# 232 small products of a zero tile at the beginning of an attention and MLP kernel

## The chip, the core and the metric

The kernel runs on one core of a Trainium2 chip. The engines are TensorE (PE in the profile: matmuls; PEld: the loading of their stationary operand), VectorE (DVE), ScalarE (ACT), GpSimd (POOL) and SyncE (SP, which issues most DMAs). Each engine takes its instructions in the order in which the program lists them. The metric is the device time of one launch in microseconds; lower is better. The median of three runs before is 1787.42 us (1785.45 to 1788.26).

## The reference, cut to what matters

The program is a chain of three layers over 8 batches of 576 rows and 512 columns: a landmark (Nyström) attention with 8 heads, a token mixer of rank 32 with an MLP, and a Fourier mixer with a normalisation and a second MLP.

```
q_lm = q.reshape(B, H, 32, 18, D).mean(axis=3);  k_lm = the same of k
A, Bm, C = sm(q, k_lm), sm(q_lm, k_lm), sm(q_lm, k)      # softmax of scaled products
Z = Bm^T / (norm1(Bm) * norminf(Bm));  6 times: Z = 2 Z - Z Bm Z
attn = A @ Z @ C @ v
u = x + (x^T U V)^T;   x1 = u + relu(u @ w_ch1) @ w_ch2
u = x1 + real(fft(fft(x1)));  un = normalised(u)
out = u + relu(un @ w_ch1') @ w_ch2'
```

Only the first few instructions of the first batch's attention lie beside the change: the means of q and k over 18 rows (the landmarks), `Bm` and `C`.

## The kernel before, in words

The whole program is one list written by hand (`tc.manual_schedule()`), so the order of the Python code is the order on each engine. The main part is matrix products of 128x512 tiles for the MLPs, three products for each pair of tiles (high times high, low times high, high times low), on PE without pause for most of the run. The attention of a batch is a chain of small steps, spread over slots between those products. For batch 0 there are no products to fill in yet: the MLP has no input until the attention of batch 0 is done. In its slots the program puts fillers (L1541 to L1543: six products of the identity with itself, read by nobody) and sums for later batches (L738).

What runs first, by engine:

- SP loads k and q of batch 0 (L719, two DMAs each), then constants, then raw weights.
- POOL fills four tiles with zeros in `attention_constants`: `v` (L664), `ETt` (L665), then `kb` and `qb` (L668). `kb` and `qb` are 128x256 tiles that hold the landmarks of k and q in a block pattern; the zeros between the blocks stay for the whole attention part.
- DVE sums k and q over 18 rows (L726, into the small tile `ls`), twice for each. After each sum POOL scales the result into `kb` or `qb` (`landmark`, L728, two instructions for each sum).
- PE then multiplies `qb` by `kb` (`Batch.kernel`, L759: eight products of a 128x32 stationary part of `qb` with a 128x32 part of `kb`, each group of four written to four different 32-row quarters of the result), and `qb` by k (`scores`, L823 and L828). DVE takes the maxima (L765, L831, L833), ACT the exponentials (L767, L837).
- POOL's next work after the landmarks is a conversion step (L69) of the token mixer's matrix U, which DVE's L71 waits for.

A product of two float32 tiles stands in the trace as two records on PE: the eight of L759 are sixteen. `mlp.bank()` hands out three PSUM banks in turn.

Of the kernel before, what the change touches and what calls it, by code (L numbers as in the profile page):

```python
# [9 lines left out]
F32 = mybir.dt.float32  # L10
# [13 lines left out]
P = 128  # L24
# [11 lines left out]
def f32(ap):  # L36
    return ap.bitcast(F32)
# [3 lines left out]
def body(ctx: ExitStack, tc: tile.TileContext, qT, kT, vn, mU, mV, w11, w12, w21, w22,  # L41
         ident, bones, istack, tabs, out):
    nc = tc.nc
# [42 lines left out]
    def fetch_raw(raw, src):  # L86
        nc.sync.dma_start(raw, src.bitcast(U32))
# [568 lines left out]
    UB = 4  # L656

    def attention_constants(cp, t):
        t["ident"] = cp.tile([P, P], F32, name="ident_sb")
        nc.sync.dma_start(t["ident"], ident)  # L660
        t["U"] = cp.tile([P, 6, R], F32, name="U_sb")
        t["v"] = cp.tile([P, 5, DM], F32, name="v_")
        t["ETt"] = cp.tile([P, 2, P], F32, name="ETt")
        nc.gpsimd.memset(t["v"][64:P, 4, :], 0.0)  # L664
        nc.gpsimd.memset(t["ETt"][64:P], 0.0)  # L665
        for nm in ("kb", "qb"):
            t[nm] = cp.tile([P, 4, 64], F32, name=nm)
            nc.gpsimd.memset(t[nm], 0.0)  # L668
        for nm, src, n in (("bones", bones, P), ("istack", istack, R)):
            t[nm] = cp.tile([P, n], F32, name=nm + "_sb")  # L670
            nc.sync.dma_start(t[nm], src)
        t["at"] = cp.tile([P, 4, S], F32, name="at")
        t["W"] = cp.tile([P, 4, 64], F32, name="W")
# [16 lines left out]
    def place_v(t):  # L690
        for n in range(3):
            src = t["vst"][R * n:R * n + R].unsqueeze(1).to_broadcast([R, 2, S // 3])
            for h in range(4):
                nc.sync.dma_start(t["at"][32 * h:32 * h + 32, 1 - h % 2:4:2, n * S // 3:(n + 1) * S // 3], src)
# [622 lines left out]
    def pool(name, **k):  # L1317
        return tc.tile_pool(name=name, bufs=1, reuse_waits="tile", **k)

    def chained(gens):  # L1320
        for g in gens:
            yield from g

    def some(gen, n):
        for _ in range(n):
            next(gen, 0)
# [156 lines left out]
    with pool("mm") as mp, pool("pm", space=PSUM) as pm:  # L1483
        mlp = Mlp(mp, pm, 3, passes)

        def direct():

            ws = [mlp.weight(nm) for nm in ("w1", "w2") for _ in range(HM)]
            raws = []
            seq = [*range(4), *range(HM, 2 * HM, 2), *range(4, HM), *range(HM + 1, 2 * HM, 2)]  # L1490

            def fetch():
                i = len(raws)
                if i < len(ws):
                    if i < EARLY:
                        raw = f32(mp.tile([P, 2, 512], F32R, name="g", bufs=HM)).rearrange(
                            "p a n -> p (a n)").bitcast(U32)
                    else:
                        raw = cv0.tile([P, 1024], U32, name="wraw", bufs=2)
                    fetch_raw(raw, srcs[0][seq[i]])  # L1500
                    raws.append(raw)

            for n in range(2):
                fetch()
                yield 1

            old = None
            for n, i in enumerate(seq):
                while len(raws) < min(max(n + 2, min(n + 3, EARLY)), len(ws)):
                    fetch()  # L1510
                new = convert(cv0, raws[n], ws[i], 2)
                for g in (new, old, old, new):
                    if g:
                        yield next(g)
                old = new
            yield from old

        EARLY = 8
        with pool("aa") as ap_, pool("ac") as ac, pool("cv0") as cv0, pool("pt", space=PSUM) as psb:
            t = {}  # L1520
            batches = [Batch(ap_, psb, t, b, mlp) for b in range(B)]
            slots = Slots()
            FIRST, GAP = -1 - Batch.LAST, 11
            half = (0, 1, 2, 4, 6, 8, 9, 10)
            for b in range(B):
                slots.add(GAP + STEPS * (b - 1) - 23 + 2 * (b == 1) if b else FIRST, batches[b].steps(batches[b + 1] if b + 1 < B else None))
            slots.add(GAP + STEPS * (B - 1) - 10, [(0, lambda: mlp.get_tail(B))])
            slots.add(GAP + STEPS * (B - 1) - 8, ((k, lambda k=k: mlp.hand_tail(B, k)) for k in range(4)))

            slots.add(FIRST, [(11, lambda: place_v(t))])  # L1530

            sums = {**{n - 11: [(1, 'k', 3 * n, 3 * n + 3)] for n in range(6)}, 3: [(2, 'k', 0, 6)], 5: [(2, 'k', 6, 12)], 7: [(2, 'k', 12, 18)]}

            def filler(s):

                if s in sums:
                    for b, nm, first, last in sums[s]:
                        batches[b].landmark_sums(nm, first, last)
                    return

                ps = mlp.bank()  # L1541
                for _ in range(6):
                    nc.tensor.matmul(ps[:, 0:P], t["ident"], t["ident"], start=True, stop=True)  # L1543

            with tc.manual_schedule():
                for what in "kq":
                    batches[0].load(what)
                attention_constants(ac, t)
                small, large = attention_setup(t, ap_, cv0), direct()
                some(small, 1)  # L1550
                some(large, 1)
                batches[0].load("v")
                some(large, 1)
                convs = chained([small, large])
                for s in range(FIRST, 0):
                    slots.run(s)
                    if s - FIRST in (6, *range(10, 20)):
                        filler(s)
                    some(convs, 0 if s < FIRST + 4 else 1 + s % 2)
                later, gen = staging(cv0, 1, 2), mlp.stream(0)  # L1560
                for s in range(N + GAP - 8):
                    if s >= GAP or s in half:
                        next(gen)
                    else:
                        filler(s)
                    slots.run(s)
                    if s < GAP + 13:
                        some(convs, 2)
                        if s == GAP + 12:
                            some(convs, 99)  # L1570
                    else:
                        some(later, 1 if s % 3 == 2 else 2)
                some(later, 999)
                some(gen, 9)
        with tc.manual_schedule():
            scales = Scales(rs)
            mlp.plan(UN, [(c, c + 1) for c in range(PLAIN, NCH, 2)], quarters)
            with pool("cv") as cv, pool("fp") as fp, pool("fc") as fc, pool("pf", space=PSUM) as psb:
                f = {}
                slots = Slots()  # L1580
                starts = (33, 58, 83, 108, 133, 157, 182, 206)
                for b, s in enumerate(starts):
                    slots.add(s, Mixer(fp, psb, f, b).steps(b + 1 == B))
                later = Pace(chained([staging_pairs(cv, (2, 3)), staging_sums(cv)]))
                gen = mlp.stream(1)
                setup = fourier_setup(f, fc, fp)

                def room(s):
                    r = s - max((a for a in starts if a <= s), default=-99)
                    return 1.45 if r > 40 else 1.4 if r in (*range(10, 21), 23, 24) else .7 if r in (4, 9, 21, 22) else 0  # L1590

                for s in range(N + 2 * PLAIN * STEPS - LEAD):
                    if s in (N, N + PLAIN * STEPS):
                        some(gen, 9)
                        gen = mlp.stream(2 + (s > N))
                    next(gen)
                    slots.run(s)
                    next(setup, 0)
                    later.step(room(s))
                later.rest()  # L1600
            assert not slots.at
            with pool("tl") as mlp.last_pool, pool("tp", space=PSUM) as mlp.last_ps:
                last = mlp.pairs(quarters, Y, scales, U2, ByChunk(y3))
                next(last)
                for s in range(LEAD):
                    next(gen)
                    next(last)
                    next(last)
                some(gen, 9)
                for _ in last:  # L1610
                    pass
# [83 lines left out]
```

## Time and profile before

| | |
|---|---|
| median of three runs | 1787.42 us |
| lowest, highest | 1785.45, 1788.26 us |
| profiled execution: its time | 1789.14 us |
| profiled execution: span of the core | 1787.4 us |
| mean granted TensorE clock | 0.997 |
| PE busy | 1757.6 us (98%) |
| DVE busy | 1171.2 us (66%) |
| POOL busy | 328.2 us (18%) |

The span goes from the core's first to its last instruction; the time of the execution is 1.7 us longer. Where the profile holds no record of the granted clock it shows 1.00: the first 15 us of this run have none, and there the durations of PE's own records must be read instead. Matmuls of one engine overlap, so the distance between starts, not the duration of one record, is what a record costs in a sequence.

### The profile page before, as it was taken

What the parts mean: (1) busy time and instruction counts of PE and PEld (TensorE: products, weight loads), DVE (VectorE), ACT (ScalarE), POOL (GpSimd) and SP (SyncE); (2) the same over time, 40 slices, a digit from 0 to 9 for tenths busy, and PEclk for the clock granted to TensorE, in tenths of its full rate; (3) what the DMA queues carried; (4) which work ended last, traced back from release to release, by engine and by line L of the source; (5) the groups of instructions that cost most, each with busy time, mean ns of one, the idle gap of its engine ahead of it and who ended that gap; (6) DMA issues with size and microseconds to landing.
All of it is one profiled execution on the core that took longest, in us unless ns stands there. A gap on an engine that the chain in (4) does not pass through costs nothing.

```text
span 1787.4 us, 30912 instructions
## 1 busy us (share of the span) xinstructions
PE 1757.6 (98%) x11905; PEld 1432.7 (80%) x11905; DVE 1171.2 (66%) x2028; ACT 735.6 (41%) x1520; POOL 328.2 (18%) x314
## 2 busy tenths in 40 slices
PE   6999999999999999999999999999999999999999
PEld 4777777777788888888878888888878888888887
DVE  7897666566322977888886665657575674577564
ACT  4554443444211333433342333434256445454642
POOL 3324211221110321211111122211111001100100
PEclk9999999999999999999999999999999999999999
DMA  7555456443536764546555954776688778878764
GB/s 254 182 174 171 152 175 206 155 162 105 179 137 249 242 234 154 183 164 216 179 179 193 329 200 148 273 281 201 222 290 273 216 243 257 261 228 247 223 214 153
DMA packets 215895, 371.00 MB, mean 208 GB/s; under 512 B 28970, under 2 KB 129930, under 8 KB 215748
## 3 DMA queue, kind: packets, MB, share of 16 engines
q1 hardware_dynamic: 211140, 359.59, 60.9%
q10 hardware_dynamic: 4608, 9.44, 1.4%
q8 instruction: 94, 1.54, 0.4%
q14 instruction: 53, 0.43, 0.1%
HBM read 262.18 MB, written 106.17 MB: 206 GB/s over the span
## 4 chain that ended last, share of the span: by engine, by line
PE 88%; DVE 7%; DMA 2%; ACT 1%; issue 1%; SPq 0%; POOL 0%; DVEq 0%; ACTq 0%
PE ps L291 9%; PE ps L293 9%; PE ps L292 9%; PE ps L238 9%; PE ps L240 8%; PE ps L239 8%; PE ps L329 7%; PE ps L331 7%; PE ps L330 7%; PE ps L554 1%; PE ps L553 1%; PE ps L555 1%; PE ps_f L77 1%; PE ps_f L76 1%; PE ps_f L75 1%
## 5 line engine op out<-in xcount | busy, mean ns | idle before, releaser
L238 PE MATMUL ps<-x,w 128*128 128x512 f32 x768 | 305.4, 398 | 0.2 <-DVE g L243 0.2
L291 PE MATMUL ps<-g,w 128*128 128x512 f32 x768 | 304.2, 396 | 0.0
L240 PE MATMUL ps<-x,w 128*128 128x512 f32 x768 | 299.8, 390 | 0.0
L293 PE MATMUL ps<-g,w 128*128 128x512 f32 x768 | 299.8, 390 | 0.0
L239 PE MATMUL ps<-x,w 128*128 128x512 f32 x768 | 299.4, 390 | 0.0
L292 PE MATMUL ps<-g,w 128*128 128x512 f32 x768 | 299.2, 390 | 0.0
L243 DVE SCALAR_TENSOR_TENSOR g<-ps,g 128x512 fp32r<-128x512 f32 x192 | 132.4, 690 | 206.7 <-ACT g L242 206.4
L242 ACT ACTIVATE g<-ps 128x512 fp32r<-128x512 f32 x192 | 114.0, 597 | 264.0 <-PE ps L240 263.4
L291 PEld LDWEIGHTS ps<-g,w 128*128 128x128 f32 x768 | 144.3, 188 | 31.9 <-issue 3.5
L240 PEld LDWEIGHTS ps<-x,w 128*128 128x128 f32 x768 | 144.1, 188 | 31.4
L293 PEld LDWEIGHTS ps<-g,w 128*128 128x128 f32 x768 | 144.1, 188 | 31.1
L238 PEld LDWEIGHTS ps<-x,w 128*128 128x128 f32 x768 | 144.3, 188 | 29.9 <-DVE g L243 0.6
L292 PEld LDWEIGHTS ps<-g,w 128*128 128x128 f32 x768 | 144.4, 188 | 27.4
L239 PEld LDWEIGHTS ps<-x,w 128*128 128x128 f32 x768 | 144.4, 188 | 26.9
L302 DVE TENSOR_TENSOR xf<-ps,xf 128x512 f32<-128x512 f32 x88 | 60.5, 687 | 86.7 <-PE ps L293 84.6
L406 ACT COPY ps<-ps 128x512 f32<-128x512 f32 x126 | 72.4, 575 | 94.4 <-PE ps L331 93.4
L51 POOL TENSOR_TENSOR stg<-cva,stg 128x512 fp32r<-128x512 f32 x48 | 65.4, 1363 | 216.8 <-ACT stg L50 190.4
L458 POOL TENSOR_TENSOR w<-w,w 128x512 f32<-128x512 f32 x24 | 33.3, 1389 | 362.1 <-DMA w<-rs 181.6
L329 PE MATMUL ps<-xs,w 128*128 128x512 f32 x240 | 94.2, 392 | 1.9 <-ACT ps L406 1.9
L331 PE MATMUL ps<-xs,w 128*128 128x512 f32 x240 | 94.1, 392 | 0.0
L330 PE MATMUL ps<-xs,w 128*128 128x512 f32 x240 | 93.9, 391 | 0.0
L51 POOL TENSOR_TENSOR x<-xf,x 128x512 fp32r<-128x512 f32 (+7 forms) x48 | 60.1, 1254 | 157.9 <-ACT x L50 122.7
(420 smaller groups left out, 3356.9 us busy)
## 6 DMA issues: line engine op xcount, KB each, us to landing
w<-e SPq DMA_DIRECT2D x84, 512.0 KB
w<-d SPq DMA_DIRECT2D x126, 256.0 KB
w<-d SPq DMA_DIRECT2D x60, 512.0 KB
wraw<-w SPq DMA_DIRECT2D x56, 512.0 KB
d<-stg SPq DMA_DIRECT2D x48, 512.0 KB
y<-xf SPq DMA_DIRECT2D x64, 256.0 KB
xf<-y SPq DMA_DIRECT2D x52, 256.0 KB
u<-u1T ACTq DMA_DIRECT2D x32, 288.0 KB
```

The lines of the kernel that those rows point to most:

```text
L51: (eng or nc.vector).tensor_tensor(lo, src, f32(hi), op=ALU.subtract)
L238: nc.tensor.matmul(ps, wh, xh, start=k == 0, stop=False)
L239: nc.tensor.matmul(ps, wl, xh, start=False, stop=False)
L240: nc.tensor.matmul(ps, wh, xl, start=False, stop=k == 3)
L242: nc.scalar.activation(g[:, 0, :], ps, AF.Relu)
L243: nc.vector.scalar_tensor_tensor(out=g[:, 1, :], in0=ps, scalar=0.0, in1=f32(g[:, 0, :]), op0=ALU.max, op1=ALU.subtract)
L291: nc.tensor.matmul(ps, wh, gh, start=k == m0, stop=False)
L292: nc.tensor.matmul(ps, wl, gh, start=False, stop=False)
L293: nc.tensor.matmul(ps, wh, gl, start=False, stop=k == m1 - 1)
L329: nc.tensor.matmul(ps, wh, xh, start=first and k == 0, stop=False, skip_group_check=True)
L330: nc.tensor.matmul(ps, wl, xh, start=False, stop=False, skip_group_check=True)
L331: nc.tensor.matmul(ps, wh, xl, start=False, stop=last and k == 1, skip_group_check=True)
```

## The change

Three things are edited. The zero fill of `qb` and `kb` moves to the head of `attention_constants`, ahead of those of `v` and `ETt`, with `qb` first. Then, after the constants and ahead of everything else that PE does, 232 products are issued. Each takes columns 0 to 31 of `qb` as the stationary operand and columns 32 to 63 as the moving one, both over 128 rows, and writes the same 32x32 corner of one PSUM bank. Nobody reads the result. `qb` holds zeros at that time.

```diff
--- before.py
+++ after.py
@@ -656,6 +656,9 @@
     UB = 4
 
     def attention_constants(cp, t):
+        for nm in ("qb", "kb"):
+            t[nm] = cp.tile([P, 4, 64], F32, name=nm)
+            nc.gpsimd.memset(t[nm], 0.0)
         t["ident"] = cp.tile([P, P], F32, name="ident_sb")
         nc.sync.dma_start(t["ident"], ident)
         t["U"] = cp.tile([P, 6, R], F32, name="U_sb")
@@ -663,9 +666,6 @@
         t["ETt"] = cp.tile([P, 2, P], F32, name="ETt")
         nc.gpsimd.memset(t["v"][64:P, 4, :], 0.0)
         nc.gpsimd.memset(t["ETt"][64:P], 0.0)
-        for nm in ("kb", "qb"):
-            t[nm] = cp.tile([P, 4, 64], F32, name=nm)
-            nc.gpsimd.memset(t[nm], 0.0)
         for nm, src, n in (("bones", bones, P), ("istack", istack, R)):
             t[nm] = cp.tile([P, n], F32, name=nm + "_sb")
             nc.sync.dma_start(t[nm], src)
@@ -1515,7 +1515,7 @@
                 old = new
             yield from old
 
-        EARLY = 8
+        EARLY, WARM = 8, 232
         with pool("aa") as ap_, pool("ac") as ac, pool("cv0") as cv0, pool("pt", space=PSUM) as psb:
             t = {}
             batches = [Batch(ap_, psb, t, b, mlp) for b in range(B)]
@@ -1546,6 +1546,9 @@
                 for what in "kq":
                     batches[0].load(what)
                 attention_constants(ac, t)
+                ps, warm = mlp.bank(), t["qb"].rearrange("p a m -> p (a m)")
+                for _ in range(WARM):
+                    nc.tensor.matmul(ps[0:32, 0:32], warm[:, 0:32], warm[:, 32:64], start=True, stop=True)
                 small, large = attention_setup(t, ap_, cv0), direct()
                 some(small, 1)
                 some(large, 1)
```

On PE before, the program begins with the products of the landmarks (`ps_b` is a PSUM bank of the attention):

```order
L759 MATMUL ps_b<-kb,qb 32x32 [waits Pool_49] x2
L759 MATMUL ps_b<-kb,qb 32x32 x2
L759 MATMUL ps_b<-kb,qb 32x32 [waits Pool_49]
L759 MATMUL ps_b<-kb,qb 32x32 x3
L823 MATMUL ps_c<-k__226,qb 32x512 [waits DMAHW0_49]
```

In the changed kernel the 232 products (`ps<-qb`) stand ahead of the same list:

```order
L1551 MATMUL ps<-qb 32x32 [waits Pool_49]
L1551 MATMUL ps<-qb 32x32 x231
L759 MATMUL ps_b<-kb,qb 32x32 [waits Pool_49] x2
L759 MATMUL ps_b<-kb,qb 32x32 x2
L759 MATMUL ps_b<-kb,qb 32x32 [waits Pool_49]
L759 MATMUL ps_b<-kb,qb 32x32 x3
L823 MATMUL ps_c<-k__605,qb 32x512 [waits DMAHW0_49]
```

All that PE had in its list before comes behind the 232 products, in the same order.

On POOL before, the zero fills and the landmark scalings read so (`ls` is the sum that DVE made):

```order
L664 MEMSET v__235 64x512
L665 MEMSET ETt 64x256
L668 MEMSET kb 128x256 [waits Pool_49]
L668 MEMSET qb 128x256
L677 MEMSET wraw 128x128
L728 ISA
L728 TENSOR_SCALAR kb<-ls 64x2x32 [waits DVE_49,Pool_49]
L728 TENSOR_SCALAR kb<-ls 64x2x32 [waits Pool_49]
L728 TENSOR_SCALAR kb<-ls 64x2x32 [waits DVE_49]
L728 TENSOR_SCALAR kb<-ls 64x2x32
L728 TENSOR_SCALAR qb<-ls 64x2x32 [waits DVE_49]
```

In the changed kernel, the same stretch:

```order
L661 MEMSET qb 128x256
L661 MEMSET kb 128x256
L667 MEMSET v__239 64x512 [waits Pool_49]
L668 MEMSET ETt 64x256
L677 MEMSET wraw 128x128
L728 ISA
L728 TENSOR_SCALAR kb<-ls 64x2x32 [waits DVE_49]
L728 TENSOR_SCALAR kb<-ls 64x2x32 [waits Pool_49]
L728 TENSOR_SCALAR kb<-ls 64x2x32 [waits DVE_49]
L728 TENSOR_SCALAR kb<-ls 64x2x32
L728 TENSOR_SCALAR qb<-ls 64x2x32 [waits DVE_49,PE_49]
```

The fill of `qb` is now POOL's first work after the start, and the first scaling into `qb` has a new wait, on PE: it overwrites what the 232 products read.

## Rows read from the trace of the kernel before

**Rows 1.** The page: busy time by engine, and the chain by engine.

```profile
PE 1757.6 (98%) x11905; PEld 1432.7 (80%) x11905; DVE 1171.2 (66%) x2028; ACT 735.6 (41%) x1520; POOL 328.2 (18%) x314
...
PE 88%; DVE 7%; DMA 2%; ACT 1%; issue 1%; SPq 0%; POOL 0%; DVEq 0%; ACTq 0%
```

**Rows 2.** Timeline of POOL: start us, us, engine, line, operation, count, [idle before <-releaser].

```profile
0.73 0.52 POOL L664 MEMSET v__235<- 64x512 f32 x1 [0.29 <-POOLq L1684]
...
1.81 0.33 POOL L668 MEMSET qb<- 128x256 f32 x1
...
8.95 0.81 POOL L728 TENSOR_SCALAR qb<-ls 64x64 f32<-64x64 f32 x2 [0.86 <-DVE ls L726]
10.42 0.85 POOL L728 TENSOR_SCALAR qb<-ls 64x64 f32<-64x64 f32 x2 [0.65 <-DVE ls L726]
```

**Rows 3.** Timeline of PE, same columns, 0 to 60 us.

```profile
9.37 0.77 PE L759 MATMUL ps_b<-kb,qb 128*32 128x32 f32 x8 [9.37 <-POOL qb L728]
11.32 0.34 PE L759 MATMUL ps_b<-kb,qb 128*32 128x32 f32 x8 [1.18 <-POOL qb L728]
11.59 1.96 PE L823 MATMUL ps_c<-k__226,qb 64*32 64x512 f32 x16
...
13.69 2.35 PE L1543 MATMUL ps<-ident_sb 128*128 128x128 f32 x12
...
23.75 0.65 PE L969 MATMUL ps_n<-ry 32*32 32x64 f32 x16 [3.75 <-DVE cva L95]
24.33 1.11 PE L851 MATMUL ps_c<-ident_sb,E 128*128 128x128 f32 x4
...
33.85 0.66 PE L928 MATMUL ps_c<-ident_sb,A 128*128 128x128 f32 x4
...
38.95 0.46 PE L951 MATMUL ps_b<-U_sb,A 128*32 128x32 f32 x32
...
42.84 1.60 PE L1543 MATMUL ps<-ident_sb 128*128 128x128 f32 x12
...
44.73 1.09 PE L823 MATMUL ps_c<-k__372,qb 64*32 64x512 f32 x16
```

**Rows 4.** The chain that ended last, 0 to 24 us: start us, us, what.

```profile
11.66 1.91 PE ps_c L823 x16
...
13.59 1.29 DVE st L831 x2
```

**Rows 5.** Timeline of DVE, columns as in rows 2.

```profile
13.21 0.15 DVE L778 TENSOR_TENSOR st<-st 128x2 f32<-128x2 f32 x1
```

**Rows 6.** One line's PE records: duration ns min/median/max, first and last start.

```profile
L951 PE MATMUL ps_b<-U_sb,A x64: 196/196/217, 38.9 to 39.6; 128*32 128x32 f32 x64
...
L1543 PE MATMUL ps<-ident_sb x60: 274/275/581, 13.7 to 55.0; 128*128 128x128 f32 x60
...
L851 PE MATMUL ps_c<-ident_sb,E x8: 421/421/474, 24.3 to 28.1; 128*128 128x128 f32 x8
...
L928 PE MATMUL ps_c<-ident_sb,A x8: 272/272/328, 33.9 to 37.0; 128*128 128x128 f32 x8
```

**Rows 7.** Windows: busy us (instructions) of PE, PEld, DVE, ACT, POOL; PEclk, DMA share, GB/s.

```profile
0.00:5.00 5.00, 0.00 (x0) 0.00 (x0) 0.58 (x1) 1.28 (x1) 1.69 (x9) 1.00 0.63 219
...
20.00:25.00 5.00, 1.25 (x19) 1.11 (x20) 4.05 (x14) 0.84 (x2) 0.00 (x0) 0.71 0.99 372
25.00:30.00 5.00, 5.00 (x37) 4.28 (x35) 4.83 (x10) 2.86 (x6) 1.32 (x1) 0.61 0.54 165
28.00:29.00 1.00, 1.00 (x7) 0.93 (x6) 0.93 (x4) 0.47 (x1) 0.00 (x0) 0.53 0.14 41
29.00:30.00 1.00, 1.00 (x6) 0.80 (x5) 0.97 (x3) 1.00 (x3) 0.00 (x0) 1.00 0.13 37
...
60.00:1787.40 1727.40, 1714.94 (x11042) 1399.84 (x11040) 1124.26 (x1917) 707.28 (x1444) 310.52 (x284) 1.00 0.62 206
```

**Rows 8.** Waits of PE after 60 us: us in total, times, longest.

```profile
PE ps_l L1255 <- DVE le L1250: 2.7, 3, 1.4
```

## The prediction, made before the run

> **What bounds the kernel now.** I read the page first: PE is busy for 98% of the span and holds 88% of the chain that ended last [rows 1]. The windows say where the rest is: PE does nothing in the first 5 us, and after 60 us it is idle for only 1727.40 - 1714.94 = 12.5 us [rows 7]. So from 60 us on PE runs almost without pause, and what moves its work of the first microseconds moves the end by about the same amount. Then the timelines of POOL and PE for the beginning, with the chain. PE's first instruction starts at 9.37 us, released by POOL's scaling into `qb`; the second half of the same eight products follows at 11.32 us, after POOL's second pair of scalings, which starts at 10.42 and takes 0.85 us [rows 2, 3]. From there the chain goes through L823 to DVE's maximum at 13.59 us [rows 4]. DVE had ended the step before it (L778) at 13.21 + 0.15 = 13.36 us [rows 5], so only 0.23 us of that stretch waits for PE alone.
>
> The clock needs a second look. In the first windows the profile shows 1.00 only because it has no record. L1543's twelve records take 2.35 us at 13.69 and 1.60 us at 42.84; L823's sixteen 1.96 us at 11.59 and 1.09 us at 44.73 [rows 3]. [...]
>
> **The change part by part.** The new zero fills cost nothing: the same five fills, with `qb` first. PE can begin when that one is done, at 0.73 + 0.33 us, and 0.05 us for the handover (POOL ends at 10.42 + 0.85 = 11.27, PE starts at 11.32): 1.11 us [rows 2, 3].
>
> How many records are 232 products? L759 has eight products and two rows of eight records [rows 3]: two records for each float32 product, so 464.
>
> [...] All 232 products use the same 32 columns of the array and the same corner of the result, so they can't run side by side; the distance between starts at one place counts. No row has it for 32 columns alone, so I bound it. L1543 runs at one place too, with 128 moving columns: (1.60 - 0.275) / 11 = 0.120 us from start to start [rows 3, 6]; with a quarter of the columns, a quarter is 0.030. L951 has my shape, 32 records in four places that overlap, so eight after each other at each: (0.46 - 0.196) / 7 = 0.038 us [rows 3, 6], which still contains the stagger of the four. Below: 0.030; above: 0.038. I take 0.032, nearer to the quarter since the stagger is in the other. At 1.2 GHz: L851 and L928 are the same four records at the two levels, (1.11 - 0.421) / 3 = 0.230 and (0.66 - 0.272) / 3 = 0.129 us [rows 3, 6], a ratio of 1.78; that makes 0.057 us.
>
> When the clock rises. All at 1.2 GHz would be 464 x 0.057 = 26.4 us, all at 2.4 GHz 14.8 us. Between them I take what the restart at 23.75 us showed, 28.94 - 23.75 = 5.2 us of work at the lower level. In it 91 records are done; 373 x 0.032 = 11.9 us remain. The last product ends at 1.11 + 5.2 + 11.9 + 0.2 (the duration of one record [rows 6]) = 18.4 us. The gap that they were to fill ends at 8.95 us, when POOL wants to write `qb` [rows 2].
>
> Who waits. The order of POOL shows the new wait: the first scaling into `qb` overwrites what the products read, so it stands until 18.4 us. Both sums of q are long there by then, so the two pairs run back to back: 0.81 + 0.85 = 1.66 us [rows 2], and the second half of L759 starts at 18.4 + 1.66 + 0.05 = 20.1 us instead of 11.32: 8.8 us late. Behind the waiting scaling in POOL's queue stands the conversion L69, which moves by the same amount with DVE's L71 behind it. DVE waits at L765 for the products of L759, with every later conversion in its queue; ACT waits for DVE. SP's load of the next batch's k waits for the score products in both kernels, and goes along. Nothing in this list is released by something that the wait leaves alone, so the delay passes whole.
>
> What comes back. [...] L823 alone would be 1.96 - 1.09 = 0.9 us faster, but DVE's L778 stands only 0.23 us ahead of the point where it waits; with 0.07 us of the shorter L759 I count 0.3 us. Later, the two groups of L851 run at 1.2 GHz between 23.75 and 28.94 us, 0.45 us each slower than L928; if the clock should stay up there this time, up to 0.9 us more comes back. DVE is busy for 4.83 of 5 us there [rows 7], so less than that, and the gap ahead of it is as long as before; I count nothing.
>
> Sum: 8.8 - 0.3 = 8.5 us. The profiled execution has a span of 1787.4 us and a time of 1789.14; its time would become 1797.6. The median of the runs is 1787.42, 1.7 us below that time, and the delay adds to it alike: 1795.9 us, 0.48% slower. The bounds: with 0.030 us and 2.4 GHz throughout, the products end at 1.11 + 13.9 + 0.2 = 15.2 us and the delay is 5.6 us; less 0.3 and 0.9 that leaves 4.4 us, 1791.8. With 0.038 us (0.068 at 1.2 GHz) and the rise after 5.2 us they end at 21.3 us: delay 11.7, less 0.3, 1798.8.
>
> **The rivals.** *The clock never rises during the products.* No row shows a rise after a run of products as small as these. Then 26.4 us at 1.2 GHz: end at 27.7, L759's second half at 29.4, 18.1 us late: 1805.5. With 0.030 x 1.78 = 0.053 us for each record it is 16.3 us and 1803.7. Against it: the records follow each other without a gap, which PE's work after 9.37 us did not do and the clock rose all the same.
>
> *The products fit into the gap, and the kernel is not slower.* L951's records start (0.46 - 0.196) / 31 = 0.0085 us apart; if products at one place could overlap as these do, 464 would end at 1.11 + 3.9 + 0.2 = 5.2 us, POOL's new wait would be met ahead of 8.95 us, and only the gains remain: 0.3 to 1.2 us, about 1786.6. The point from which it decides is (8.95 - 1.11 - 0.2) / 464 = 0.0165 us for each record. Against it: L1543 at one place needs 0.120 us for four times the columns, and at four times 0.0165 it would need 0.066. [...]
>
> *The delay is absorbed later.* If PE's later waits were for something that the delay doesn't move, they would shrink. After 60 us PE is idle for 12.5 us in all; the largest group, for DVE at L1255, is 2.7 us in three waits [rows 7, 8], and DVE's own work moves along. Were half of the 12.5 us free to give, 8.5 - 6.2 = 2.3 us would be left: 1789.7.
>
> **How the numbers follow.** Forecast, a clear delay with a rise of the clock on the way: 0.76; its own range is 1791.8 to 1798.8. Slow clock throughout: 0.10. Products that fit: 0.08. Absorbed: 0.06. What a measurement of this kernel can tell from no change is about 0.2%, or 3.6 us: 1783.8 to 1791.0. Products that fit come out inside that band, but for a part of 0.02 if much more comes back from the clock than I count (faster); absorbed lies inside too: 0.12 for no change in all, and 0.76 + 0.10 = 0.86 for slower. The range reaches up to the lower price of the slow clock, 1804, and down to the edge of the band, 1791; it leaves out most of the last two rivals.
>
> **What would show it.** PE's first record at about 1.1 us; 464 records of the new line, the distance between them first 0.05 to 0.07, then 0.030 to 0.038 us; the last one at 16 to 21 us. POOL's first scaling into `qb` starts right after it, with a wait of 7 to 12 us put down to PE. L759's second half starts some 9 us later than 11.32, L823 takes about 1.1 us, and PE's idle time after 60 us stays near 12.5 us. The forecast is wrong if the products end ahead of 10 us, if POOL does not wait for them, or if PE's work at 60 us is not late by what L759 was.

## The result, and the profile after

The changed kernel is slower: a median of 1801.73 us (1800.56 to 1805.2, five runs) against 1787.42 (1785.45 to 1788.26, five runs), a ratio of 1.0084 with a 95% interval from 1.0070 to 1.0098. That is 14.3 us; the forecast was 8.5, a time of 1795.9, in a range of 1791 to 1804. The profiled execution took 1800.56 us with a span of 1798.8, against 1789.14 and 1787.4. These two traces are thus only 11.4 us apart: the one before took longer than any of the five runs before, the one after is the fastest of its five.

PE's timeline of the changed kernel begins so (columns as in [rows 3]):

```profile
1.10 9.26 PE L1551 MATMUL ps<-qb 128*32 128x32 f32 x223 [1.10 <-POOL qb L661]
10.78 7.79 PE L1551 MATMUL ps<-qb 128*32 128x32 f32 x241 [0.42 <-issue]
19.07 0.25 PE L759 MATMUL ps_b<-kb,qb 128*32 128x32 f32 x2 [0.50 <-POOL qb L728]
19.51 0.26 PE L759 MATMUL ps_b<-kb,qb 128*32 128x32 f32 x6 [0.20 <-POOL qb L728]
20.38 0.26 PE L759 MATMUL ps_b<-kb,qb 128*32 128x32 f32 x7 [0.61 <-POOL qb L728]
21.52 0.19 PE L759 MATMUL ps_b<-kb,qb 128*32 128x32 f32 x1 [0.88 <-issue]
21.64 1.09 PE L823 MATMUL ps_c<-k__226,qb 64*32 64x512 f32 x16
...
22.99 2.83 PE L1543 MATMUL ps<-ident_sb 128*128 128x128 f32 x12
26.70 0.46 PE L792 MATMUL ps_b<-dg,bones_sb 128*128 128x128 f32 x2 [0.89 <-ACT E L839]
27.09 1.10 PE L896 MATMUL ps_c<-kb,q__229 128*32 128x64 f32 x64
...
30.25 0.43 PE L969 MATMUL ps_n<-ry 32*32 32x64 f32 x16 [0.54 <-DVE ry L809]
...
33.81 0.43 PE L969 MATMUL ps_n<-ry 32*32 32x64 f32 x16 [1.11 <-DVE ry L974]
...
42.77 0.38 PE L936 MATMUL ps_b<-ident_sb,A 128*64 128x128 f32 x2 [1.51 <-DVE A L922]
...
47.81 0.46 PE L951 MATMUL ps_b<-U_sb,A 128*32 128x32 f32 x32
...
49.36 0.26 PE L955 MATMUL ps_b<-U_sb,A 128*32 128x32 f32 x4 [0.69 <-issue]
...
54.50 1.09 PE L823 MATMUL ps_c<-k__605,qb 64*32 64x512 f32 x16
```

The products run from 1.10 us, and the second row of them ends at 10.78 + 7.79 = 18.57 us. L759's second half, at 11.32 us before [rows 3], starts at 20.38, and its last record stands apart at 21.52 with 0.88 us of idle time that nothing in the profile releases ("issue"). L823 takes 1.09 us, as at the full clock, against 1.96 before [rows 3]. L792 starts at 26.70, 9.7 us later than in the kernel before:

```profile
17.00 0.46 PE L792 MATMUL ps_b<-dg,bones_sb 128*128 128x128 f32 x2 [0.96 <-ACT E L839]
```

POOL's timeline (same columns) shows the new wait:

```profile
5.88 0.81 POOL L728 TENSOR_SCALAR kb<-ls 64x64 f32<-64x64 f32 x2 [3.49 <-DVE ls L726]
7.27 0.81 POOL L728 TENSOR_SCALAR kb<-ls 64x64 f32<-64x64 f32 x2 [0.58 <-DVE ls L726]
18.65 1.68 POOL L728 TENSOR_SCALAR qb<-ls 64x64 f32<-64x64 f32 x4 [10.58 <-PE ps L1551]
```

The four scalings into `qb` that started at 8.95 and 10.42 us [rows 2] run in one piece from 18.65 us, after 10.58 us of waiting for the products.

The clock, by windows of PE's records (columns as in [rows 7]):

```profile
5.00:6.00 1.00, 1.00 (x23) 1.00 (x22) 0.96 (x2) 0.00 (x0) 0.12 (x1) 1.00 1.01 378
6.00:7.00 1.00, 1.00 (x36) 1.00 (x34) 1.00 (x1) 0.00 (x0) 0.61 (x2) 1.00 1.01 406
7.00:8.00 1.00, 1.00 (x37) 1.00 (x35) 0.26 (x2) 0.00 (x0) 0.65 (x2) 1.00 1.01 410
...
23.00:24.00 1.00, 1.00 (x13) 1.00 (x6) 0.97 (x5) 0.00 (x0) 0.00 (x0) 0.56 0.06 16
24.00:25.00 1.00, 1.00 (x7) 1.00 (x7) 0.96 (x5) 0.00 (x0) 0.00 (x0) 0.50 0.76 124
```

23 records lie in the sixth microsecond, 36 and 37 in the next two: the rise came near 6 us, 4.9 us after PE's first record. From 18.57 to 21.52 us PE was idle for 0.50 + 0.20 + 0.61 + 0.88 = 2.19 us, and in the windows from 23 to 25 us the grant is 0.56 and 0.50: L1543 took 2.83 us at 22.99, against 2.35 at 13.69 before [rows 3].

### The profile page after: what moved, and what is told of

Same layout as the page of the kernel before. It is cut to its first block, busy times and chain, and to the rows that moved or that the text cites. A ratio compares the mean times of both kernels' runs of the same rounds, so it can differ in the third digit from the quotient of the medians.

```text
span 1798.8 us, 31840 instructions
## 1 busy us (share of the span) xinstructions
PE 1772.8 (99%) x12369; PEld 1447.7 (80%) x12369; DVE 1170.5 (65%) x2028; ACT 736.1 (41%) x1520; POOL 328.9 (18%) x314
## 3 DMA queue, kind: packets, MB, share of 16 engines
q8 instruction: 97, 1.59, 0.4%
## 4 chain that ended last, share of the span: by engine, by line
PE 85%; DVE 8%; DMA 3%; issue 2%; ACT 1%; SPq 0%; ACTq 0%; POOL 0%; DVEq 0%; POOLq 0%
PE ps L291 9%; PE ps L293 9%; PE ps L292 9%; PE ps L238 8%; PE ps L240 8%; PE ps L239 8%; PE ps L329 7%; PE ps L330 7%; PE ps L331 7%; PE ps L553 1%; PE ps L555 1%; PE ps L554 1%; PE ps_f L77 1%; PE ps_f L76 1%; PE ps_f L75 1%
## 5 line engine op out<-in xcount | busy, mean ns | idle before, releaser
L238 PE MATMUL ps<-x,w 128*128 128x512 f32 x768 | 305.6, 398 | 1.3 <-DVE g L243 1.3
L238 PEld LDWEIGHTS ps<-x,w 128*128 128x128 f32 x768 | 144.3, 188 | 31.6 <-DVE g L243 2.1
```

The costliest lines, as they stand in the source:

```text
L238: nc.tensor.matmul(ps, wh, xh, start=k == 0, stop=False)
```

## The experiments

The forecast covers the delay of L759; some 5 us more had to be explained. Theory 1: the delay is all there is. Theory 2: PE runs out of instructions at certain places of its list, and a list that is longer at the front moves these places to others, where they cost more or less. What suggested it are the idle times put down to "issue" in the timeline above (10.78, 21.52, 49.36 us). Such an idle time of PE is called a stop below. Every experiment is the changed kernel with one edit. The differences below are medians against the runs of the kernel before that went with them on the same chip (1786.85 us for the first four, 1788.15 for the next four, 1787.71 for the last three).

**A zero tile of its own.**

```diff
+        t["zero"] = cp.tile([P, 64], F32, name="zero_sb")
+        nc.gpsimd.memset(t["zero"], 0.0)
...
-                ps, warm = mlp.bank(), t["qb"].rearrange("p a m -> p (a m)")
+                ps, warm = mlp.bank(), t["zero"]
```

> The 232 products read a zero tile of their own, so POOL's scalings into qb wait for DVE's sums alone again; PE's list is unchanged. Theory 1 (the delay of L759 passes to the end): the products still end near 18.4 us, L759's second half starts at about 18.5 instead of 20.4, and of the 14 us about 1.7 come back: 1800. Theory 2 (places where PE runs out of instructions, moved by the longer list, make a good part of the 14 us): the list is as long as in the changed kernel, so these stay; also about 1800. Rival (the wait of POOL is the main cost): near 1790.

Measured: 1803.20 us, 16.4 above before (ratio 1.0089, 1.0076 to 1.0103). POOL no longer waits: its last scalings into `qb` start at 11.07 us. PE's timeline (L761 is L759 here, L1553 the products):

```profile
15.07 3.71 PE L1553 MATMUL ps<-zero_sb 128*32 128x32 f32 x112 [0.34 <-issue]
18.59 0.23 PE L761 MATMUL ps_b<-kb,qb 128*32 128x32 f32 x3
...
18.64 0.30 PE L761 MATMUL ps_b<-kb,qb 128*32 128x32 f32 x12
20.72 0.19 PE L761 MATMUL ps_b<-kb,qb 128*32 128x32 f32 x1 [1.78 <-issue]
```

PE comes to L759 at 18.6 us, as expected, and does the first 15 of its 16 records at once; the sixteenth waits 1.78 us for "issue" and starts at 20.72 us, against 21.52 in the changed kernel. Taking away one wait brought nothing that the times show, since another stood behind it. Both theories had 1800 us here, so this run doesn't tell them apart; what is out is the rival, 1790.

**Four places.**

```diff
-                for _ in range(WARM):
-                    nc.tensor.matmul(ps[0:32, 0:32], warm[:, 0:32], warm[:, 32:64], start=True, stop=True)
+                for n in range(WARM):
+                    sl = slice(32 * (n % 4), 32 * (n % 4) + 32)
+                    nc.tensor.matmul(ps[sl, 0:32], warm[:, 0:32], warm[:, 32:64], start=True, stop=True,
+                                     skip_group_check=True)
```

> The same 232 products and 464 records, but written in turn to four places of 32 rows of the bank, so that they can overlap as those of L951 do: one record each 0.0133 us at the lower clock instead of 0.053. They should end at 6 to 8 us, ahead of POOL's first scaling into qb at 8.95. Theory 1 (shift): no delay is left and L823 runs at the full clock: 0.3 to 1.2 us below before, 1786 to 1787. Theory 2 (the longer instruction list costs by itself): still 2 to 5 us above before, 1789.5 to 1792.5, with PE idle without a releaser at the places where the changed kernel has it.

Measured: 1797.17 us, 10.3 above before (1.0052, 1.0040 to 1.0065), above the ranges of both theories. The expectation that the products would end by 8 us was wrong, and PE's timeline shows why (L1552 is the line of the products):

```profile
1.10 3.21 PE L1552 MATMUL ps<-qb 128*32 128x32 f32 x223 [1.10 <-POOL qb L661]
8.50 1.93 PE L1552 MATMUL ps<-qb 128*32 128x32 f32 x128 [4.20 <-issue]
12.23 1.73 PE L1552 MATMUL ps<-qb 128*32 128x32 f32 x113 [1.80 <-issue]
14.49 0.78 PE L759 MATMUL ps_b<-kb,qb 128*32 128x32 f32 x8 [0.53 <-POOL qb L728]
15.80 0.33 PE L759 MATMUL ps_b<-kb,qb 128*32 128x32 f32 x7 [0.54 <-POOL qb L728]
17.05 0.21 PE L759 MATMUL ps_b<-kb,qb 128*32 128x32 f32 x1 [0.92 <-issue]
```

The records overlap as hoped: 223 of them take 3.21 us, against 9.26 in the changed kernel. Then PE stands for 4.20 us, does 128, stands for 1.80, does 113, and 15 of L759's 16, which make 128 again. The sixteenth, at 17.05 us, comes after another stop, so L759 ends 5.6 us later than before (its last record there starts at 11.41). The steps are 223, 128 and 128 records; I read them as a list that reaches PE in blocks. On the DMA queues, between 4.3 and 8.6 us of this kernel (queue, packets, MB, share):

```profile
q1 hardware_dynamic: 759, 1.64, 101.3%
q8 instruction: 1, 0.02, 1.4%
```

One packet stands on the instruction queue there, from 6.18 to 7.14 us by the trace; PE goes on at 8.50, 1.4 us after its end. The next two packets end at 10.98 and 15.87 us, 1.2 us ahead of the records at 12.23 and 17.05. It is so in the other traces too, in all the stops that this text shows: PE goes on 1.2 to 1.7 us after a packet of this queue has ended (in the changed kernel 1.25 us at 10.78, 1.26 at 21.52, 1.40 at 49.36). The page counts 94 of them, 1.54 MB, in the kernel before and 97, 1.59 MB, in the changed one: 16.4 KB each. PE has 11905 and 12369 records on these pages, so there is one packet for 127 and for 128 of them, which agrees with the steps of 128. The packet is no longer for the other queue's load: it takes 0.96 us here, beside 101.3%, and 1.08 us at 19.18 us of the changed kernel, where that queue has 4.4% (window from 19 to 22 us). Whether that load makes it start later, no view shows.

In the kernel before, the sixteen records each of L759, L823 and L828, twelve of L1543, two of L792, 64 of L896, sixteen of L806, 64 of L896 and sixteen of L903 make 222 ahead of L969, where PE stood idle for 3.75 us [rows 3]. The profile put that wait down to DVE; its place, at the end of the first 222 or 223 records, and a packet of the instruction queue that ends at 22.28 us, 1.5 us before PE goes on, say that it was the same stop.

**34 long products.**

```diff
-        EARLY, WARM = 8, 232
+        EARLY, WARM = 8, 34
...
-                    nc.tensor.matmul(ps[0:32, 0:32], warm[:, 0:32], warm[:, 32:64], start=True, stop=True)
+                    nc.tensor.matmul(ps[0:32, 0:256], warm[:, 0:32], warm, start=True, stop=True)
```

> 34 products of 256 moving columns instead of 232 of 32, into the same place, from the same qb: 68 records instead of 464, at 0.427 us each at the lower and 0.22 at the higher clock, so they end near 18.4 us as well, and POOL waits as in the changed kernel. Theory 1 (shift): the same delay of L759 and the same end as the changed kernel, 1799 to 1803. Theory 2 (the longer list costs by itself): PE's list is 396 records shorter, so the stops for instructions fall elsewhere, and the time differs from the changed kernel by 2 us or more, in either direction; if the stop of PE before L969 (3.1 us in the kernel before) comes back, upwards.

Measured: 1796.78 us, 9.9 above before (1.0058, 1.0044 to 1.0071), 5 us under the changed kernel. L759's second half is 8.3 us late:

```profile
19.62 0.27 PE L759 MATMUL ps_b<-kb,qb 128*32 128x32 f32 x8 [0.61 <-POOL qb L728]
```

In the whole trace no wait of PE is put down to "issue". With nearly the same delay, a list that is 396 records shorter and no stop, the time is close to what the delay alone gives. Theory 1 had 1799 at least; theory 2 had the difference of 2 us or more.

**80 products.** The edit is `WARM = 80`.

> 80 products instead of 232: at 0.053 us until about 6 us and 0.032 after it, 160 records end near 8.2 us, ahead of POOL's first scaling into qb at 8.95. Theory 1 (shift): nothing waits, L823 runs at the full clock, 0.3 to 1.2 us below before: 1786 to 1787. Theory 2 (the place of the stops for instructions counts): off from that by up to 3 us in either direction, without a delay of L759.

Measured: 1794.20 us, 7.4 above before (1.0042, 1.0029 to 1.0055), though nothing waits for the products: they end by 8.8 us and L759's second half starts at 11.46. Theory 1 is out as the whole; the time is also above the 3 us that theory 2 allowed. PE stands here in L896, ahead of its last 16 records:

```profile
23.76 0.43 PE L896 MATMUL ps_c<-kb,q__229 128*32 128x64 f32 x16 [3.48 <-issue]
```

**64, 48 and 256 products, and none.** The edits are `WARM = 64`, `48`, `256` and `0`.

> 64 products instead of 232: 128 records, which end near 7.2 us, ahead of POOL's scaling at 8.95. The traces so far show PE's first stop for instructions after 223 records and later ones in steps of 128; 128 additional records leave each stop of the kernel before at the same place of the program (the one of 3 us ahead of L969 too, beside DVE's work). Theory 2 (the places of the stops make the rest of the loss): as before, less the gain of the clock: 1785.5 to 1788.5. Theory 3 (any products at the beginning cost some 7 us, as the 80 did without a delay of L759): 1792 to 1795.

Measured: 1787.39 us (ratio 0.9999, 0.9990 to 1.0008): no difference. PE's timeline has the stop of the kernel before at the same place of the program, with the same 3.75 us, and L823 takes 1.96 us again, so the full clock is not won either:

```profile
1.10 6.43 PE L1551 MATMUL ps<-qb 128*32 128x32 f32 x128 [1.10 <-POOL qb L661]
...
12.12 0.34 PE L759 MATMUL ps_b<-kb,qb 128*32 128x32 f32 x8 [1.24 <-POOL qb L728]
12.38 1.96 PE L823 MATMUL ps_c<-k__226,qb 64*32 64x512 f32 x16
...
24.67 0.65 PE L969 MATMUL ps_n<-ry 32*32 32x64 f32 x16 [3.75 <-DVE cva L95]
```

> 48 products: 96 records, end near 6.1 us. [...] Theory 2: PE starts L969 near 20.6 us instead of 23.75, most of which DVE's work beside it hides: 1784.5 to 1788. Theory 3 (any products cost): 1790 to 1794.

Measured: 1789.30 us, 1.2 above before (1.0013, 1.0004 to 1.0021), between the ranges of theory 2 (up to 1788) and theory 3 (from 1790). L969 did start early, at 21.28 us, but L951 got a stop of 0.89 us later.

> 256 products instead of 232, 512 records or four steps of 128. They end 1.5 us later than the 232, near 19.9 us, so L759 is later still, about 10.5 us against before. Theory 1 (the delay alone): 1.5 us above the changed kernel, 1802 to 1804.5. Theory 2 (places of the stops): these are back at the program's places of the kernel before, and only the delay is left: 1796 to 1799, less than with 232.

Measured: 1799.96 us, 11.8 above before (1.0066, 1.0054 to 1.0078), 2.5 us nearer to before than the 232 products, with L759 later:

```profile
10.77 4.21 PE L1551 MATMUL ps<-qb 128*32 128x32 f32 x128 [0.20 <-issue]
15.60 4.21 PE L1551 MATMUL ps<-qb 128*32 128x32 f32 x128 [0.62 <-issue]
20.98 1.20 PE L1551 MATMUL ps<-qb 128*32 128x32 f32 x33 [1.16 <-issue]
...
24.00 0.33 PE L759 MATMUL ps_b<-kb,qb 128*32 128x32 f32 x8 [0.61 <-POOL qb L728]
```

Its second half starts at 24.00 us, 12.7 late, 2 us more than I had expected, since the products themselves are stopped three times. The time lies between the ranges of the two theories: about 1 us above theory 2's, with that longer delay, and 2 us below theory 1's. The stop ahead of L969 is back, but short.

> No products; what is left of the change is the order of the zero fills on POOL, and the turn of the PSUM banks by one. All theories: as before, 1786 to 1788.5. If it were above 1790, the order of the fills would carry part of the loss.

Measured: 1787.55 us (0.9995, 0.9987 to 1.0004): the order of the zero fills costs nothing.

**16, 40 and 56 products.** The edits are `WARM = 16`, `40` and `56`.

> 16 products: 32 records, under 2 us of PE's work, over by 3 us; nothing waits for them. The stops for instructions move by a quarter of a step, as with the 80 products (160 records are one step and a quarter): PE should run dry in the second group of L896, near 20 us, and stand until about 23.7 with DVE waiting. Theory 2 (the places of the stops): most of what the 80 cost, 3 to 8 us above before, 1791 to 1796. If the cost goes with the number or the time of the products: as before, 1786 to 1789.

Measured: 1791.76 us, 4.1 above before (1.0022, 1.0013 to 1.0031), from 32 records that are over by 3.02 us. PE's timeline, and then DVE's:

```profile
1.10 1.92 PE L1551 MATMUL ps<-qb 128*32 128x32 f32 x32 [1.10 <-POOL qb L661]
...
11.47 0.34 PE L759 MATMUL ps_b<-kb,qb 128*32 128x32 f32 x8 [1.10 <-POOL qb L728]
...
18.82 0.88 PE L896 MATMUL ps_c<-kb,q__229 128*32 128x64 f32 x48
23.35 0.43 PE L896 MATMUL ps_c<-kb,q__229 128*32 128x64 f32 x16 [3.66 <-issue]
...
47.59 1.73 PE L1543 MATMUL ps<-ident_sb 128*128 128x128 f32 x8 [1.49 <-issue]
```

```profile
23.85 0.69 DVE L908 TENSOR_REDUCE sm<-ps_c 128x16 f32<-128x512 f32 x1 [3.15 <-PE ps_c L896]
...
25.18 0.15 DVE L844 TENSOR_TENSOR st<-st 128x2 f32<-128x2 f32 x1
```

The stop falls where it was expected: after 48 of the 64 records, the place at which the 80 products have it. DVE's next maximum needs the other 16, so DVE stands 3.15 us. Its L844, at 21.79 us in the kernel before, starts at 25.18. A second stop, of 1.49 us, follows in L1543.

> 40 products: 80 records, over near 5.5 us, so L759 is not delayed. 464 records are three steps and 80 records, so the later stops stand at the same places of the program as in the changed kernel (the second half of L955 near 40 us of the kernel before, L903 near 236 us). Theory 2: what the changed kernel lost beyond the delay of L759 (14.3 less 9 to 10 us) appears here without the delay: 3 to 6 us above before, 1790.5 to 1794. If the loss beyond the delay comes from the delay itself: as before, 1786 to 1789.

Measured: 1790.43 us, 2.7 above before (1.0012, 1.0003 to 1.0021), just below theory 2's 3 to 6 and outside the other range. By their count the 40 products put the later stops where the 232 have them, since 464 records are three steps of 128 and 80; what is left over the whole steps is called the phase here. That phase costs without the delay, but about half of what I expected. Of the two places that I gave, L955 has no idle time here; L903 has its stop:

```profile
238.53 0.41 PE L903 MATMUL ps_b<-kb,q__2740 128*32 128x64 f32 x11 [0.81 <-issue]
```

> 56 products: 112 records, over near 6.4 us. One more phase of the stops: PE should run dry in L851 behind the first L969, where DVE is still busy with its own work, so most of the stop is hidden. Theory 2: between 1 us below and 3 us above before, 1786 to 1791, with a stop near 21 us on PE. If the cost goes with the number of products: between those of 48 and 64, 1787 to 1789.5.

Measured: 1789.80 us, 2.1 above before (1.0012, 1.0003 to 1.0020). PE stops in the first L969, for 2.24 us, a little ahead of the place that I gave; both readings allow the time. The cost does not grow with the number of products: 16 cost 4.1 us, 40 cost 2.7, 48 cost 1.2, 64 nothing, 80 cost 7.4. The phase alone doesn't give the size either: 16 and 80 products are one whole step apart. Both stop in L896 and in L1543, and at L896 near 236 us both are late by nearly the same against the run without products, 3.6 and 3.4 us. What their medians differ by, 3.3 us, comes later; their traces (spans of 1792.0 and 1792.8 us) hardly show it.

## Why the forecast was right, and where its size was off

The changed kernel is slower by the mechanism that was forecast: the products outlast the gap, POOL waits for them, and the delay passes on. That the time lies in the stated range is luck all the same: 1801.73 is above the 1798.8 at which the forecast's own story ended, and the range reached up to 1804 only for the slow clock, which did not come.

- PE's start, the records and their price were right. The 464 records begin at 1.10 us (1.11 forecast). At the full clock 128 of them take 4.21 us in the run with 256 products, (4.21 - 0.196) / 127 = 0.032 us each, as forecast. The rival that they fit into the gap is out, with a last product at 18.57 us against 8.95. A product, which is two records, takes 0.063 us.
- The rise of the clock was taken as 5.2 us after the start and measured at about 4.9. The 5.2 us run from the restart at 23.75 us of the kernel before to 28.94, where the grants put the rise: 0.50 up to 28 us, a mean of 0.53 from 28 to 29, then 1.00 [rows 7]. No run shows the clock in GHz, by which the forecast's sums name its two levels; what the runs show are grants of 0.50 and 1.00, and products at 0.054 and later 0.032 us a record. The line of the windows ahead of those two:

```profile
27.00:28.00 1.00, 1.00 (x19) 0.83 (x12) 1.00 (x2) 0.21 (x1) 0.45 (x1) 0.50 0.59 131
```

- The end of the products, 18.4 us forecast, is 18.57. The slow clock throughout is out.
- POOL's wait and the delay of L759 were forecast at 8.8 us and measured at 20.38 - 11.32 = 9.06.
- The gain was forecast at 0.3 us. DVE's L765 (11.72 us before) is 10.0 us late and its L831 9.7, which is the 0.3. L765 is later than L759's 9.06 by the stop ahead of L759's last record, so 0.9 us come on top of the delay here. In DVE's timeline after, L778 (13.21 before [rows 5]) stands right ahead of L831 (13.59 before [rows 4]):

```profile
21.75 0.22 DVE L765 TENSOR_REDUCE st<-ps_b 128x2 f32<-128x64 f32 x1 [8.86 <-PE ps_b L759]
...
23.23 0.15 DVE L778 TENSOR_TENSOR st<-st 128x2 f32<-128x2 f32 x1
23.30 1.28 DVE L831 TENSOR_REDUCE st<-ps_c 128x1 f32<-128x512 f32 x2
```

- **The step that fell short is the sum.** "So the delay passes whole" took the rest of PE's list as unchanged in cost; the term for a longer list was zero. It is measured in two ways. With the stops at the same places of the program as before, 256 products cost 11.8 us for a delay of 12.7, and 64 cost nothing. With the stops elsewhere, 80 products cost 7.4 us and 16 cost 4.1 with no delay at all. For the 232 products the delay of 9.06 us leaves 14.3 - 9.1 = 5.2 us. The 40 products, with the phase of the 232, show 2.7 us, of which up to 1.05 may be their L759 (its second half starts at 12.37).
- *The stop before L969.* In the kernel before, most of it costs nothing, since DVE's work beside it takes as long. In the changed kernel it is gone, and L969 starts only 30.25 - 23.75 = 6.5 us later, so 3.2 of the 9.7 us come back on PE. But then PE waits for DVE where it did not before: 1.11 us for L974 at 33.81 and 1.51 us for L922 at 42.77. By L951 the delay is 47.81 - 38.95 = 8.9 us, and with L955's stop it is 9.8 at L823 of the next batch (54.50 against 44.73). The second gain that the prediction named, L851 at the full clock, came and went in the same waits: its four records take 0.65 us at 30.61 instead of 1.11. I had read the 3.75 us as an idle gap without asking what ended it.
- *Absorbed later* is out. After 60 us PE had 12.5 us of idle time in the kernel before [rows 7], in the changed one it has 1738.80 - 1722.94 = 15.9 (1.3 of them a wait of L1011 that lay ahead of 60 us before). Nothing of the delay is gone at the end.
- *Where the rest comes in.* The trace of the run without products is the better measure here, since its time (1787.55 us) is that of the median; its span is 1785.8 us, 13.0 less than the changed kernel's. At L896 near 236 us (236.08 against 245.26) the changed kernel is 9.2 us behind it, about the delay alone, so what the stop at L759's last record added has been made good by then. Three steps follow, and most of the rest is in them. One is the stop in L903, which makes it 10.2:

```profile
247.21 0.41 PE L903 MATMUL ps_b<-kb,q__2932 128*32 128x64 f32 x11 [0.75 <-issue]
```

The next is L238, where PE waits 0.90 us for DVE, which makes it 11.0 (935.79 against 924.78); there DVE's L1127 has waited for a load. This wait of PE stands, with 0.78 to 0.90 us, in the four traces of this phase (the changed kernel, the zero tile of its own, the four places and the 40 products) and in none of the other nine. The third is L1202, a wait of 1.47 us for DVE against 0.23 without products, which makes it 12.6 (1039.47 against 1026.92); it differs from trace to trace and does not go with the phase.
- Open: how the phase of the stops reaches that load 900 us later, why L1202 waits, and the 1.3 us by which the medians (14.3) are further apart than these traces (13.0). That the stops are waits for the next block of the list is my reading of their spacing, of the number of the packets and of the packet that ends ahead of each; no run slowed or sped these packets, and when one is asked for no view shows.

## What to carry to other kernels

Before putting anything in front of a list that waits, ask who overwrites what it reads (POOL waited 10.58 us here), and how long it takes at one place of the array at the clock that it starts with (here 0.054 us a record at first, by the 16 products, and 0.032 later). Count instructions, not time alone: here 16 products at the front, over by 3.02 us, were followed by stops at other places and a loss of 4.1 us, while 64 products left the stop ahead of L969 where it was and cost nothing. And a wait that no view explains, at a fixed count of records, may be such a stop, whatever engine the profile names: in these traces a packet on the instruction queue ended 1.2 to 1.7 us before PE went on.

## What was not expected of the hardware

- In the run with four places PE stopped after 223 records, after 128 more and after another 128. The longest stops were 4.20 us there, 3.75 in the kernel before, 3.66 with 16 products and 3.48 with 80, each over 1.4 to 1.5 us after a packet of the instruction queue had ended.
- Products at one place cost about 0.053 us for each record ahead of the rise of the clock and 0.032 after it (the 32 records of the 16 products: (1.92 - 0.24) / 31 = 0.054). The first 223 records of the changed kernel, with the rise in them, took 9.26 us; the same number at four places took 3.21.
- 32 records that nobody waits for, over by 3.02 us, made a program of 1788 us 0.22% slower.
